# Top-k attention with a mixture of depths: seven parts for the candidates, the 24th candidate as the bias, and the checks of the bounds on VectorE

## The chip, the core and the metric

The kernel runs on one NeuronCore of a Trainium2 chip. A core has four engines that compute, each with its own queue of instructions: TensorE (matrix products, PE in the profile, with its weight loads as PEld), VectorE (DVE), ScalarE (ACT) and GpSimd (POOL). SyncE (SP) issues most of the transfers. The engines wait for each other by semaphores. The metric is the time of one execution on the device in microseconds (us), the median of several runs; lower is better.

## The reference

Eight batches with eight heads, 576 tokens and 64 values a head. Each query keeps its 32 highest scores; all others get no weight. The result, 512 values a token, is the input of a mixture of depths: in each batch the 128 tokens with the highest gate score go through a small network.

```python
scores = scale * np.matmul(q, k.transpose(0, 1, 3, 2))
kth = np.partition(scores, -top_k, axis=-1)[..., -top_k:-top_k + 1]
mask = scores >= kth
scores = np.where(mask, scores, -1000000000.0)
scores = scores - np.max(scores, axis=-1, keepdims=True)
attn = np.exp(scores)
attn = attn / (np.sum(attn, axis=-1, keepdims=True) + 1e-09)
return np.matmul(attn, v).astype(np.float32)
...
for b in range(B):
    top_idx = np.argpartition(-scores[b], capacity)[:capacity]
    xe = x[b, top_idx]
    h = np.maximum(xe @ w1, 0.0)
    ye = h @ w2
    g = 1.0 / (1.0 + np.exp(-scores[b, top_idx]))
    out[b, top_idx] = x[b, top_idx] + g[:, None] * ye
```

## The kernel before

The work is cut into 144 **units**, 18 a batch. A unit is 128 queries for two heads: a tile `sc` of 128 rows with two halves (one a head) of 576 scores. The last 64 tokens of a batch are folded so that two units take them for all heads.

The loop `for n in range(-1, N)` (L1083) is a software pipeline written out by hand. In iteration n, TensorE multiplies queries and keys of unit n + 1, VectorE searches unit n, ScalarE and GpSimd prepare unit n - 1, VectorE finds the 32nd score of unit n - 2, ScalarE and GpSimd make the mask of unit n - 3, and TensorE turns unit n - 4, adds the mask to it, and, once ScalarE has taken the exp, multiplies with v. Each engine carries out its instructions in the order in which the program lists them, since `InOrder` keeps it; queues such as `vector_late` and `pool_late` hold small pieces back until a named point of the iteration.

How the 32nd score of a row is found:

- `find_bound(sc)` (L383), VectorE. Each half is cut into 8 parts of 72 scores. A MAX8 takes the 8 highest of each part: 64 **candidates** (`cand`). Then three rounds pick the 8 highest among the candidates: the first looks at the 3 highest of each part, the second at 7, the third at all 8. After the first and the second, a match_replace overwrites what was picked. The last value of the third round, `best[2][:, i, 7]`, is the 24th candidate, at or below the row's 24th score.
- `cut(best, at)` (L413), ScalarE. A cast copies the upper 16 bits of the two 24th candidates of a unit into `seen[:, 0, ...]`: the value truncated, so a little lower.
- `part(i, sc, at, sides)` (L420), ScalarE. A sign activation of bias - (1 + 2^-23) x score, where the bias is what `cut` kept. It gives -1 for scores at or above the bound and +1 below it; the sum over a row goes to `seen[:, 2, ...]`, and shows how many scores lie above.
- In `what_is_below(n)` (L1056), GpSimd multiplies scores and signs into `y`, so that only those below the bound stay positive, and `fill` (L435) appends eight values that depend on the row's sum.
- `find_kth` (L444), VectorE. One MAX8 over the 584 values of `y`, whose 8th is the 32nd score of the row. The results of a batch lie in one tile, `next8s[b]`.
- `mask` (L449): ScalarE takes one half, GpSimd the other (in a few units VectorE).

Since `fill` only has room for up to eight values, a row may have 24 to 31 scores at or above its bound. At the end the kernel checks (`sure`, L1243) for all rows together: that the bounds and 32nd scores are above a least value, that the row sums lie in range, and some more. To this end `mask_of` (L1073) lets GpSimd copy the 36 values of a batch's 32nd scores to `seen[:, 1, ...]` once a batch. If any check fails, `general` (L1315), a slow exact path for any input, computes all batches again after the rest.

The mixture of depths of batch b runs in steps between the units of the batches b + 1 and b + 2, at places listed in `mix_at` (L991). Most steps put matmuls into TensorE's queue (`h_ps`, `y_ps`).

Of the kernel before, what the change touches and what calls it, by code (L numbers as in the profile page):

```python
# [11 lines left out]
ALU = mybir.AluOpType  # L12
FP32 = mybir.dt.float32
BF16 = mybir.dt.bfloat16
I32 = mybir.dt.int32
# [11 lines left out]
LEAST = 1.0e-16 * SMALLER  # L27
# [2 lines left out]


J = 4


class InOrder:
# [11 lines left out]
def kernel(  # L47
# [12 lines left out]
    P = nc.NUM_PARTITIONS  # L60
    B, H, S, D = q.shape
    HD = H * D
    F = moe_w1.shape[1]
    NHP = H // 2
    NT = J + 1
    JP = J * P
# [9 lines left out]
    const = ctx.enter_context(tc.tile_pool(name="const", bufs=1))  # L76
# [3 lines left out]
    wkpool = ctx.enter_context(tc.tile_pool(name="wk", bufs=2))  # L80
    stats = ctx.enter_context(tc.tile_pool(name="stats", bufs=6))
# [28 lines left out]
    for i in range(2):  # L110
        gate = const.tile([P, NT], FP32, name=f"gate{i}")
        nc.gpsimd.memset(gate, 0.0)
        parts = const.tile([P, NT, 2, 3], BF16, name=f"parts{i}")
# [13 lines left out]


    NS = B * 2 * (J * NHP + NHP // 2)
    seen = const.tile([P, 3, NS], FP32, name="seen")  # L130
    sums = const.tile([P, B * NT, H], FP32, name="sums")
    nc.gpsimd.memset(sums, 1.0)

    MIDDLE = S - 2 * (TOP_K - 8) + 1
# [245 lines left out]
            )  # L380
        return sc

    def find_bound(sc):  # L383

        w = S // 8
        cand = wkpool.tile([P, 2, 64], FP32, name="cand")
        best = [stats.tile([P, 2, 8], FP32, name=f"best{r}") for r in range(3)]  # L390
        for i in range(2):

            if i == 1:
                flush_vector()
            for u in range(8):
                dve.max(cand[:, i, 8 * u : 8 * u + 8], sc[:, i, u * w : (u + 1) * w])


        parts = cand.rearrange("p i (u e) -> p i u e", u=8)
        for r, e in enumerate((3, 7, 8)):  # L400
            for i in range(2):
                dve.max(best[r][:, i, :], parts[:, i, :, 0:e])
            if r < 2:
                for i in range(2):
                    dve.match_replace(
                        parts[:, i, :, 0:e],
                        best[r][:, i, :],
                        parts[:, i, :, 0:e],
                        LOWEST,
                    )  # L410
        return best[2]

    def cut(best, at):  # L413

        act.copy(
            out=seen[:, 0, at : at + 2],
            in_=best.rearrange("p i e -> p (i e)").bitcast(BF16)[:, 15:32:16],
        )

    def part(i, sc, at, sides):  # L420

        act.activation(
            sides[:, i, :],
            sc[:, i, :],
            AF.Sign,
            bias=seen[:, 0, at + i : at + i + 1],  # L430
            scale=-(1.0 + 2.0**-23),
            accum_out=seen[:, 2, at + i : at + i + 1],
        )

    def fill(y, at):  # L435

        pool.tensor_tensor(
            y[:, :, S : S + 8],
            steps,
            seen[:, 2, at : at + 2].unsqueeze(2).to_broadcast([P, 2, 8]),  # L440
            ALU.subtract,
        )

# [542 lines left out]
    per_batch = sum(groups(t) for t in range(NT))  # L986
# [48 lines left out]
    loading = iter(())  # L1035
    inverting = normalised = None
    of_batch = {}
    scs, bests, ys, next8s, masks = {}, {}, {}, {}, {}

    def is_unit(n):  # L1040
        return 0 <= n < N
# [1 line left out]
    def weigh(sc, tr, av, less):  # L1043
# [9 lines left out]

        return pT, last, exp

    def what_is_below(n):  # L1056
        at, sc = 2 * n, scs[n]
        cut(bests.pop(n), at)
        sides = wkpool.tile([P, 2, S], BF16, name="sides")
        y = wkpool.tile([P, 2, S + 8], FP32, name="y")  # L1060
        for i in range(2):
            part(i, sc, at, sides)
            pool.tensor_tensor(y[:, i, 0:S], sc[:, i, :], sides[:, i, :], ALU.mult)
        fill(y, at)
        ys[n] = y

    def kth_of(n):
# [2 lines left out]
            next8s[b] = stats.tile([P, per_batch, 2, 8], FP32, name="next8", bufs=2)  # L1070
        find_kth(ys.pop(n), next8s[b][:, i, :, :])

    def mask_of(n, on=None):  # L1073
        b, i = divmod(n, per_batch)
        masks[n] = mask(scs[n], next8s[b][:, i, :, :], on)
        if i == per_batch - 1:
            at = 2 * per_batch * b
            pool.tensor_copy(
                out=seen[:, 1, at : at + 2 * per_batch].rearrange("p (n i) -> p n i", i=2),
                in_=next8s.pop(b)[:, :, :, 7],  # L1080
            )

    for n in range(-1, N):  # L1083
        b, i = divmod(n, per_batch)
        if i == 0 and 0 <= b < B - 1:
            qkv[b + 1] = room_for_qkv(b + 1)
            loading = chain(
                loading, Rows(k[b + 1], q[b + 1], *qkv[b + 1][0:2]).parts()
            )
        if 0 < n + 1 < NHP:  # L1090
            turn_pair(first_rows, n + 1)
        if n == 1:
            load_v(v[0], qkv[0][2])
        if n == NHP:
            load_weights()


        gating = normalised
        if inverting is not None:
            normalised = inverting[0:2]  # L1100
            vector_late.insert(0, lambda a=inverting: normalise(*a))
            inverting = None
        else:
            normalised = None
        if gating is not None:
            vector_late.append(lambda a=gating: gates(*a))

        if is_unit(n - 4):  # L1110
            tr, av = room_to_turn()
            pT, last, exp = weigh(scs.pop(n - 4), tr, av, masks.pop(n - 4))
            exp()
        if is_unit(n - 3):
            mask_of(n - 3, (act, None) if n in scatter_steps else None)
        flush()
        if is_unit(n + 1):
            b, t, g = units[n + 1]
            ps = room_for_scores()
            multiply(t, g, *qkv[b][0:2], ps)  # L1120
            b, i = divmod(n, per_batch)
            loads = list(islice(loading, first_loads[i] if b == 0 else loads_at[i]))
            halves = [ps[:, a, :, HALF : HALF + P] for a in range(2)]
            for load, half in zip(loads, halves):
                load[0](half)
            scs[n + 1] = keep(ps, n == -1)
            for load, half in zip(loads, halves):
                load[1](half)
        if is_unit(n - 4):
            b4, t4, g4 = units[n - 4]  # L1130
            values(t4, g4, pT, last, av, qkv[b4][2])
            if n in place_steps:
                values_bank[0] = av
                next(mixtures[place_steps[n]])
            if g4 == 0:
                xs = xpool.tile([P, H, DE], FP32, name="xs")
                if t4 == 0:
                    x = xpool.tile([P, NT, HD], FP32, name="x")
                    pg = gates_of[b4 % 2]
                    of_batch[b4] = x, pg  # L1140
            keep_values(t4, g4, av, xs)
            if g4 == groups(t4) - 1:
                inverting = b4, t4, xs
                n4 = R if t4 == J else P
                keep_sums(n4, xs, sums[0:n4, b4 * NT + t4, :])
            while kept:
                kept.pop(0)()


        if is_unit(n):  # L1150
            bests[n] = find_bound(scs[n])
        flush_vector()
        flush_pool()
        if is_unit(n - 2):
            kth_of(n - 2)
        while after_kth:
            after_kth.pop(0)()


        if is_unit(n - 1):  # L1160
            what_is_below(n - 1)

        if gating is not None:
            b, t = gating
            if t == J:
                store(out[b], of_batch[b][0])
                mixtures[b] = mixture(float(b * S), of_batch[b][1], ranks[:, b, :])
        for b in mix_steps.get(n, ()):
            next(mixtures[b], None)
        b, i = divmod(n, per_batch)  # L1170
        if i == v_at and 0 <= b < B - 1:
            load_v(v[b + 1], qkv[b + 1][2])
# [67 lines left out]
    next(closed)  # L1240


    sure = stats.tile([P, 1], FP32, name="sure")  # L1243
    dve.memset(sure, 1.0)
    for what, op, than, limit in (
        (seen[:, 0, :], ALU.min, ALU.is_gt, LEAST),
        (seen[:, 1, :], ALU.min, ALU.is_gt, LEAST),
        (seen[:, 2, :], ALU.max, ALU.is_lt, float(MIDDLE)),
        (seen[:, 2, :], ALU.min, ALU.is_gt, float(MIDDLE - 16)),
        (sums.rearrange("p t h -> p (t h)"), ALU.min, ALU.is_gt, FEWEST),  # L1250
        (sums.rearrange("p t h -> p (t h)"), ALU.max, ALU.is_lt, MOST),
    ):
        far = stats.tile([P, 1], FP32, name="far")
        dve.tensor_reduce(out=far, in_=what, axis=mybir.AxisListType.X, op=op)
        dve.scalar_tensor_tensor(
            out=sure, in0=far, scalar=limit, in1=sure, op0=than, op1=ALU.mult
        )
# [133 lines left out]
```

## Time and profile before

| | |
|---|---|
| time, median of 3 runs | 844.89 us (844.6 to 846.16) |
| the profiled execution: its own time, its span | 845.82 us, 844.0 us |
| TensorE: busy, share of the span | 793.1 us, 94% |
| VectorE | 805.4 us, 95% |
| ScalarE | 759.5 us, 90% |
| GpSimd | 729.6 us, 86% |
| granted TensorE clock, mean | 0.992 |
| MAX8 of 72 scores: number, mean of one | 2304, 218 ns |
| ScalarE's truncating cast: number, mean of one | 144, 203 ns |
| GpSimd's copy to `seen`: number, mean of one | 8, 239 ns |

The times of a group of instructions are those from the start to the end of each. Instructions of one engine can overlap: the next starts before the one before has ended. The mean of one is therefore not what an engine loses to it; that is read from the starts in the timeline. A row of waits names who waited, for whom, how long in total, how often, and the longest.

The profile in 40 equal slices, busy tenths:

```profile
PE   6898888998999999999999999999999999999987
PEld 5666666666787778877787777877788777867754
DVE  7899999999999999999999999999999999999960
ACT  4799999999999999999999999999999999979831
POOL 3689889989989899999999999999999999989831
```

All four engines are busy nearly throughout; the first slices wait for the first loads, and the last four hold the end of the last batch, where one thing follows another.

### The profile page before, as it was taken

What the parts mean: (1) busy time and instruction counts of PE and PEld (TensorE: products, weight loads), DVE (VectorE), ACT (ScalarE), POOL (GpSimd) and SP (SyncE); (2) the same over time, 40 slices, a digit from 0 to 9 for tenths busy, and PEclk for the clock granted to TensorE, in tenths of its full rate; (3) what the DMA queues carried; (4) which work ended last, traced back from release to release, by engine and by line L of the source; (5) the groups of instructions that cost most, each with busy time, mean ns of one, the idle gap of its engine ahead of it and who ended that gap; (6) DMA issues with size and microseconds to landing.
All of it is one profiled execution on the core that took longest, in us unless ns stands there. A gap on an engine that the chain in (4) does not pass through costs nothing. (4 is left out here: it accounts for less than half of the span.)

```text
span 844.0 us, 28167 instructions
## 1 busy us (share of the span) xinstructions
PE 793.1 (94%) x9887; PEld 612.4 (73%) x9887; DVE 805.4 (95%) x4905; ACT 759.5 (90%) x1701; POOL 729.6 (86%) x730
## 2 busy tenths in 40 slices
PE   6898888998999999999999999999999999999987
PEld 5666666666787778877787777877788777867754
DVE  7899999999999999999999999999999999999960
ACT  4799999999999999999999999999999999979831
POOL 3689889989989899999999999999999999989831
PEclk9699999999999999999999999999999999999999
DMA  8931111411141221511323221412215102101021
GB/s 171 279 75 29 40 64 26 104 45 35 58 97 28 52 40 58 110 40 27 89 37 82 51 47 56 101 30 52 39 58 110 27 2 76 23 2 27 2 70 30
DMA packets 122134, 50.38 MB, mean 60 GB/s; under 512 B 116416, under 2 KB 116416, under 8 KB 120960
## 3 DMA queue, kind: packets, MB, share of 16 engines
q1 hardware_dynamic: 118672, 43.91, 21.6%
q0 software_dynamic: 1728, 4.20, 2.8%
q8 instruction: 80, 1.31, 0.7%
q14 instruction: 70, 0.57, 0.3%
q10 hardware_dynamic: 1584, 0.39, 0.2%
HBM read 36.93 MB, written 11.55 MB: 57 GB/s over the span
## 5 line engine op out<-in xcount | busy, mean ns | idle before, releaser
L43 POOL TENSOR_TENSOR y<-sc,sides 128x576 f32<-128x576 f32 x288 | 365.0, 1288 | 73.1 <-ACT sides L43 70.0
L43 DVE MAX8 cand<-sc 128x8 f32<-128x72 f32 x2304 | 330.9, 218 | 1.7 <-ACT sc L43 1.7
L43 POOL TENSOR_SCALAR less<-sc,next 128x576 bf16<-128x576 f32 x135 | 232.9, 1725 | 3.2 <-DVE next L43 2.5
L43 ACT ACTIVATE sides<-sc,seen 128x576 bf16<-128x576 f32 x288 | 221.0, 768 | 5.2
L43 PE MATMUL ptr<-out_of_reach,less 128*128 128x128 bf16 x1136 | 204.8, 220 | 16.2 <-POOL less L43 16.0
L43 PE MATMUL ptr<-ident,sc 128*128 128x128 f32 x1136 | 214.4, 279 | 0.0
L43 DVE MAX8 next<-y 128x8 f32<-128x584 f32 x288 | 204.4, 751 | 3.2 <-POOL y L43 3.2
L43 PE MATMUL ps<-kT,qT 64*128 64x288 f32 (+1 forms) x1280 | 180.9, 431 | 7.6 <-ACT qT L43 5.8
L43 PEld LDWEIGHTS av<-v,pT 128*64 128x64 f32 x4544 | 144.1, 137 | 46.3 <-ACT last L43 33.7
L43 PEld LDWEIGHTS ptr<-ident,sc 128*128 128x128 f32 x1136 | 160.8, 142 | 22.4 <-PE av L43 8.7
L43 PE MATMUL av<-v,pT 128*64 128x65 f32 x4544 | 163.7, 224 | 13.8 <-ACT last L43 12.2
L43 ACT COPY sc<-ps 128x1152 f32<-128x1152 f32 (+1 forms) x144 | 160.5, 1114 | 8.5 <-PE ps L43 7.2
L43 ACT ACTIVATE pT<-ptr 128x1024 f32<-128x1024 f32 x142 | 144.1, 1015 | 18.1 <-PE ptr L43 14.6
L43 PEld LDWEIGHTS <-less 128*128 128x128 bf16 x1296 | 133.2, 104 | 36.4 <-POOL less L43 21.8
L43 DVE MAX8 best<-cand 128x8 f32<-128x24 f32 (+2 forms) x864 | 142.4, 201 | 0.1
L43 PEld LDWEIGHTS ps<-kT,qT 64*128 64x128 f32 (+1 forms) x1280 | 97.8, 177 | 46.6 <-issue 22.1
L43 ACT ACTIVATE less<-sc,next 128x576 bf16<-128x576 f32 x143 | 110.6, 774 | 6.5 <-DVE next L43 6.3
L43 DVE MATCH_REPLACE8 cand<-best,cand 128x24 f32<-128x24 f32 (+1 forms) x576 | 101.9, 185 | 0.0
L43 PE MATMUL av<-vpair,last 128*128 128x130 f32 (+1 forms) x314 | 68.1, 317 | 0.0
L43 PE MATMUL h_ps<-xeT,w 128*128 128x128 f32 x464 | 61.6, 277 | 0.0
L43 PEld LDWEIGHTS h_ps<-xeT,w 128*128 128x128 f32 x464 | 56.0, 192 | 2.1 <-issue 1.2
L43 PE MATMUL y_ps<-w,hT 128*128 128x512 f32 x112 | 56.7, 601 | 0.0
(129 smaller groups left out, 869.7 us busy)
## 6 DMA issues: line engine op xcount, KB each, us to landing
v<-in_v_dram SPq DMA_DIRECT2D x64, 128.0 KB, 3.3
out_dram<-x SPq DMA_DIRECT2D x8, 1024.0 KB, 4.1
rows<-in_k_dram SPq DMA_DIRECT2D x56, 128.0 KB, 2.9
rows<-in_q_dram SPq DMA_DIRECT2D x56, 128.0 KB, 3.1
w<-in_moe_w_dram SPq DMA_DIRECT2D x2, 2048.0 KB
gate_row<-row_dram SPq DMA_DIRECT2D x7, 288.0 KB, 5.1
w<-in_k_dram SPq DMA_DIRECT2D x8, 128.0 KB, 3.4
last<-in_k_dram SPq DMA_DIRECT2D x8, 128.0 KB, 3.5
```

What stands on the lines that cost most here:

```text
L43: return lambda *a, **kw: self._tc.keep_in_program_order(fn(*a, **kw))
```

## The change

- The candidates come from 7 parts (`PARTS`) of 82 or 83 scores in place of 8 of 72: 56 candidates. The three rounds look at 3, 7 and 8 of each part as before.
- The third round writes into a tile `bound` with the values of a whole batch. `part` takes the 24th candidate from it, untruncated, as its bias; `cut` and its cast are gone.
- `keep_least`, once a batch on VectorE, takes the least of the batch's bounds, of its 32nd scores, and of a bit test of the bounds, which shows a bound whose lower 23 bits are exactly 1 (a sign of 0 could occur there). GpSimd's copy in `mask_of` is gone. For the last batch it runs at the end, ahead of the check.
- The check reduces the 8 values of each of these in place of 288; `seen` keeps the row sums alone.

```diff
-    def find_bound(sc):
-        w = S // 8
-        cand = wkpool.tile([P, 2, 64], FP32, name="cand")
-        best = [stats.tile([P, 2, 8], FP32, name=f"best{r}") for r in range(3)]
+    def find_bound(sc, bound):
+        cand = wkpool.tile([P, 2, 8 * PARTS], FP32, name="cand")
+        best = [stats.tile([P, 2, 8], FP32, name=f"best{r}") for r in range(2)]
+        best.append(bound)
...
-            for u in range(8):
-                dve.max(cand[:, i, 8 * u : 8 * u + 8], sc[:, i, u * w : (u + 1) * w])
+            for u in range(PARTS):
+                dve.max(
+                    cand[:, i, 8 * u : 8 * u + 8],
+                    sc[:, i, u * S // PARTS : (u + 1) * S // PARTS],
+                )
...
-        act.copy(
-            out=seen[:, 0, at : at + 2],
-            in_=best.rearrange("p i e -> p (i e)").bitcast(BF16)[:, 15:32:16],
-        )
...
-            bias=seen[:, 0, at + i : at + i + 1],
+            bias=bound[:, i, 7:8],
             scale=-(1.0 + 2.0**-23),
-            accum_out=seen[:, 2, at + i : at + i + 1],
+            accum_out=seen[:, at + i : at + i + 1],
...
+    def bound_of(n):
+        b, i = divmod(n, per_batch)
+        if i == 0:
+            bounds[b] = stats.tile([P, per_batch, 2, 8], FP32, name="bound", bufs=2)
+        find_bound(scs[n], bounds[b][:, i, :, :])
...
+    def keep_least(b, bound, kth):
+        low = stats.tile([P, per_batch, 2], I32, name="low", bufs=1)
+        dve.tensor_scalar(
+            out=low,
+            in0=bound.bitcast(I32),
+            scalar1=(1 << 23) - 1,
+            scalar2=1,
+            op0=ALU.bitwise_and,
+            op1=ALU.bitwise_xor,
+        )
+        for w, of in enumerate((bound, kth, low)):
+            dve.tensor_reduce(
+                out=least[:, w, b : b + 1], in_=of, axis=mybir.AxisListType.XY, op=ALU.min
+            )
...
-        if i == per_batch - 1:
-            at = 2 * per_batch * b
-            pool.tensor_copy(
-                out=seen[:, 1, at : at + 2 * per_batch].rearrange("p (n i) -> p n i", i=2),
-                in_=next8s.pop(b)[:, :, :, 7],
-            )
+        if i == per_batch - 1 and b < B - 1:
+            keep_least(b, bounds.pop(b)[:, :, :, 7], next8s.pop(b)[:, :, :, 7])
...
+    keep_least(B - 1, bounds.pop(B - 1)[:, :, :, 7], next8s.pop(B - 1)[:, :, :, 7])
...
-        (seen[:, 0, :], ALU.min, ALU.is_gt, LEAST),
-        (seen[:, 1, :], ALU.min, ALU.is_gt, LEAST),
-        (seen[:, 2, :], ALU.max, ALU.is_lt, float(MIDDLE)),
-        (seen[:, 2, :], ALU.min, ALU.is_gt, float(MIDDLE - 16)),
+        (least[:, 0, :], ALU.min, ALU.is_gt, LEAST),
+        (least[:, 1, :], ALU.min, ALU.is_gt, LEAST),
+        (least[:, 2, :], ALU.min, ALU.is_gt, 0.5),
+        (seen, ALU.max, ALU.is_lt, float(MIDDLE)),
+        (seen, ALU.min, ALU.is_gt, float(MIDDLE - 16)),
```

More of the change, by code (lines that the diff above doesn't have):

```diff
@@ L32 @@
 J = 4
+PARTS = 7
 class InOrder:
@@ L129 @@
     NS = B * 2 * (J * NHP + NHP // 2)
-    seen = const.tile([P, 3, NS], FP32, name="seen")
+    seen = const.tile([P, NS], FP32, name="seen")
+    least = const.tile([P, 3, B], FP32, name="least")
     sums = const.tile([P, B * NT, H], FP32, name="sums")
@@ L394, in find_bound @@
                 flush_vector()
-            for u in range(8):
-                dve.max(cand[:, i, 8 * u : 8 * u + 8], sc[:, i, u * w : (u + 1) * w])
-        parts = cand.rearrange("p i (u e) -> p i u e", u=8)
+            for u in range(PARTS):
[3 more added lines that the diff above has]
+                )
+        parts = cand.rearrange("p i (u e) -> p i u e", u=PARTS)
         for r, e in enumerate((3, 7, 8)):
@@ L410, in find_bound, with part @@
                     )
-        return best[2]
-    def cut(best, at):
-        act.copy(
-            out=seen[:, 0, at : at + 2],
-            in_=best.rearrange("p i e -> p (i e)").bitcast(BF16)[:, 15:32:16],
-        )
-    def part(i, sc, at, sides):
+    def part(i, sc, bound, at, sides):
         act.activation(
@@ L439, in fill @@
             steps,
-            seen[:, 2, at : at + 2].unsqueeze(2).to_broadcast([P, 2, 8]),
+            seen[:, at : at + 2].unsqueeze(2).to_broadcast([P, 2, 8]),
             ALU.subtract,
@@ L1037 @@
     of_batch = {}
-    scs, bests, ys, next8s, masks = {}, {}, {}, {}, {}
+    scs, bounds, ys, next8s, masks = {}, {}, {}, {}, {}
     def is_unit(n):
@@ L1054, in weigh @@
         return pT, last, exp
+    def bound_of(n):
[3 more added lines that the diff above has]
+        find_bound(scs[n], bounds[b][:, i, :, :])
     def what_is_below(n):
         at, sc = 2 * n, scs[n]
-        cut(bests.pop(n), at)
+        b, i = divmod(n, per_batch)
+        bound = bounds[b][:, i, :, :]
         sides = wkpool.tile([P, 2, S], BF16, name="sides")
@@ L1061, in what_is_below @@
         for i in range(2):
-            part(i, sc, at, sides)
+            part(i, sc, bound, at, sides)
             pool.tensor_tensor(y[:, i, 0:S], sc[:, i, :], sides[:, i, :], ALU.mult)
@@ L1150 @@
         if is_unit(n):
-            bests[n] = find_bound(scs[n])
+            bound_of(n)
         flush_vector()
```

## The prediction

> **What bounds the kernel now.** I read the busy row first, then a table of busy time over four stretches, then the waits of TensorE in the same stretches, then single units in the timeline. The table (length, then busy time of each engine with its number of instructions, granted clock, DMA share, GB/s):
>
> ```profile
> 40.00:215.00 175.00, 156.38 (x2097) 119.38 (x2096) 173.44 (x1065) 167.81 (x379) 159.23 (x152) 1.00 0.23 52
> 215.00:740.00 525.00, 516.89 (x6552) 403.07 (x6553) 523.13 (x3228) 504.63 (x1136) 483.99 (x472) 1.00 0.24 56
> 740.00:800.00 60.00, 56.90 (x720) 45.09 (x719) 59.86 (x364) 51.90 (x115) 53.85 (x51) 1.00 0.06 11
> ```
>
> The columns are PE, PEld, DVE, ACT, POOL. VectorE is full in all three. That alone would say that every nanosecond taken from VectorE counts. But TensorE stands at 89% in the first stretch and 98.5% in the second. Its waits, first in 40 to 215 us, then in 215 to 740 us (total, times, longest):
>
> ```profile
> PE ptr L43 <- POOL less L43: 14.9, 25, 1.3
> PE av L43 <- ACT last L43: 2.8, 5, 0.9
> ```
> ```profile
> PE av L43 <- ACT last L43: 7.5, 12, 0.9
> ```
>
> In the first stretch TensorE lost 17.7 us to others; in the second, three times as long, 7.5 us, which is nearly all of its 525 - 516.9 = 8.1 us of idle time. A busy TensorE could still be one with stretched matmuls, so I looked at two successive units:
>
> ```profile
> 439.21 1.24 PE L43 MATMUL ps<-kT,qT 64*128 64x288 f32 x8
> 440.38 0.44 PE L43 MATMUL ps<-ident,rows 128*128 128x128 f32 x2
> 440.75 1.15 PE L43 MATMUL av<-v,pT 128*64 128x65 f32 x32
> 441.83 0.49 PE L43 MATMUL av<-vpair,last 128*128 128x130 f32 x2
> 442.16 1.05 PE L43 MATMUL h_ps<-xeT,w 128*128 128x128 f32 x8
> ...
> 444.68 1.24 PE L43 MATMUL ps<-kT,qT 64*128 64x288 f32 x8
> 445.85 0.44 PE L43 MATMUL ps<-ident,rows 128*128 128x128 f32 x2
> 446.22 1.15 PE L43 MATMUL av<-v,pT 128*64 128x65 f32 x32
> 447.30 0.49 PE L43 MATMUL av<-vpair,last 128*128 128x130 f32 x2
> 447.63 1.05 PE L43 MATMUL h_ps<-xeT,w 128*128 128x128 f32 x8
> ```
>
> The steps from start to start are 1.17, 0.37, 1.08, 0.33 in both, and 5.47 us from unit to unit. Such equal steps are those of an engine that runs at its own pace. From about 215 us on, when the expert's h and y matmuls of batch 0 join in, TensorE therefore limits most units, and VectorE the same to within 1.5%: **two bounds lie on top of each other**. Before 215 us there are no such matmuls, and VectorE is the bound alone.
>
> **VectorE, searching.** In a unit it now runs 16 MAX8 of 72 elements:
>
> ```profile
> 339.61 1.42 DVE L43 MAX8 next<-y 128x8 f32<-128x584 f32 x2
> 340.94 2.24 DVE L43 MAX8 cand<-sc 128x8 f32<-128x72 f32 x16
> 343.09 0.31 DVE L43 MAX8 best<-cand 128x8 f32<-128x24 f32 x2
> ```
>
> Start to start, 16 take 343.09 - 340.94 = 2.15 us, 134 ns each; a MAX8 of 584 takes (340.94 - 339.61)/2 = 665 ns. So an element costs (665 - 134)/512 = 1.04 ns. With seven parts there are 14 MAX8 of 82 or 83 elements, 134 + 10.3 x 1.04 = 145 ns: 2.03 us, 0.12 us less. The three selecting rounds read 21, 49 and 56 instead of 24, 56 and 64, and the two replacing ones 21 and 49: 28 elements less for each of two halves, 0.058 us. Together **0.18 us a unit**, 25.5 us over 144 units. Here a rule of the Trainium skill gives another sum: "VectorE: DVE Perf Modes", section "The DRAIN you can't avoid", has the next instruction wait until the pipeline is empty. Then whole durations count: 16 x 218 ns (the row's mean) against 14 x 229 is 0.28 us, 49 us in all with the rounds. The row shows 218 ns long instructions starting 134 ns apart, and I take the row.
>
> **VectorE, checking.** Each batch adds a bitwise tensor_scalar and three reductions of 36 elements. Reductions in the trace: 142 ns for 6 elements, 186 for 40; small tensor_scalars 102 to 154. Four make 0.5 to 0.7 us; I take 0.6, no wait, since VectorE made all inputs itself a unit before. What no row shows is a bitwise operation or a reduction on int32. Nearest are two int32 casts, 351 ns for 128 elements and, once, 4095 ns for 16. I take the short one's side, for the long one came once at the start. Nothing can be gained below zero here.
>
> **ScalarE.** 144 casts go. One holds its engine from 344.19 to 344.40, 0.21 us; in other units up to 0.28. The sign activation then waits for VectorE itself. That wait is covered: from the last MAX8 of the selection to the sign it is 3 to 6 us in the units from 24 on that I compared. If it were late, the next unit's exp, queued behind the sign, and TensorE's values after it would be late by as much. ScalarE falls from 96% busy by 3.7%.
>
> **GpSimd** loses 8 copies of 0.24 us, one a batch: 0 to 2 us, I take 0, since it waits longer for ScalarE in every batch. **DMA queues and TensorE** keep every instruction and place.
>
> **The end.** The four reductions of 288 with their products (0.55 us each, start to start) become two, and three of 8 (about 0.25), plus the last batch's 0.6: 2.2 becomes 2.5 us. That runs from 818.8 us beside the gather of xe, which frees TensorE at 822.7; the sum must be ready at 823.3, after the transposes, and is today at 822.9. The 0.3 us about fits; if that cover fails, 0 to 0.3 us, I take 0.
>
> **The sum, against the profile's own 844.0 us span (845.8 with what lies around it; the runs' median is 844.9, 0.1% less, so I take the differences off the median).**
> - To 215 us: units 0 to 5 wait for the first loads, some 31 units are VectorE's. 31 x 0.18 - 0.6 = **4.9 us**. Between 3 and 5.5: others get in the way, or not.
> - 215 to 740: TensorE can give back only its idle 8.1 us. It waits for the last exp of a unit, and ScalarE comes late to it after two or three crowded units without a pause. Each carried one cast: 2 x 0.2 off waits of 0.6 and 0.7 us, 60% of 7.5 is **4.7 us**. Between 1.5 and 8.1.
> - 740 to 800: TensorE's idle 3.1 us; I take **1.2**, from 0 to 3.1.
> - After 800 us nothing changes.
>
> 10.8 us: 844.9 - 10.8 = **834.1**. What is late next is TensorE, and VectorE will begin to wait.
>
> A second rule is to be weighed here, since it speaks for more: "Perfetto Trace Analysis", section "Identifying the Most-Contended Engine", says that matmul busy time is a bad measure and that TensorE's headroom is judged by the busy share of its weight loads. That is 403/525 = 77% in the long stretch, so TensorE would have a quarter to spare and VectorE's saving would count whole. The repeated 5.47 us say that there is none, whatever keeps it busy, and I go by them.
>
> **Rivals.**
> - *VectorE alone sets the pace* (the second rule is right). 25.5 - 1.1 for the first six units - 7 x 0.6 = 20.2 us: **824.7**. For it: VectorE's idle time is 1.9 us in 525. Against: the equal steps. Chance 0.15.
> - *Only the first stretch gains*: waits for the last exp turn out to be bounded by the transposes, not by ScalarE's casts. 844.9 - 4.9 = **840.0**. For it: ScalarE too waited for TensorE's transposes. Against: ScalarE runs without a pause in the units in question. Chance 0.14.
> - *The other side: the integer check is slow.* Its place is VectorE's queue ahead of a unit's search; its price the 4.1 us of the one slow int32 cast, for two instructions a batch. A batch then adds 8.5 us and saves 3.2, so VectorE is 42 us longer: **887**. It decides from 3.2 us a batch, 1.4 an int32 instruction. Against: the other int32 cast at 0.35. Chance 0.04.
> - *The change doesn't do what it says*: with seven parts the 24th candidate lies lower, and one row with over 31 scores at or above it sends all batches through the general path at the end, after 844 us. That path's eight MAX8 of 576 a unit, some 0.66 us each, are 0.76 ms over 144 units alone, so past **1600**. I counted on the reference's inputs: the fullest row has 31. Chance 0.01.
>
> **How the numbers follow.** Forecast 0.66, the rest as above. The range from 826.5 to 840.2 holds the forecast's own (16.7 us of gain at most, 4.5 at least: 828.2 to 840.4), the second rival, and part of the first; outside are the rest of the first, the slow check, and a gain still smaller: under 2 in 10. This kernel's runs tell 0.2%, 1.7 us, from no change. Every case but the last two gains more than that; the forecast at its worst leaves 0.03 for a smaller one. Faster 0.92, same 0.03, slower 0.05.
>
> **What would show it.** TensorE above 99% busy from 215 to 740 us with the same 5.47 us units; VectorE with idle time there of some 2%, waiting for ScalarE's scores or GpSimd's y; 14 MAX8 about 145 ns apart; the first 215 us shorter by about 5. It is wrong if TensorE's units shrink below 5.44 us (the first rival), if its waits for the last exp stay at 7 us (the second), or if an int32 instruction takes over 1 us.

## The result and the profile after

| | before | after |
|---|---|---|
| time, median of 4 runs each | 845.25 us (844.6 to 846.16) | 837.33 us (835.55 to 837.57) |
| ratio, with its 95% interval | | 0.9901 (0.9884 to 0.9918) |
| span of the profiled execution | 844.0 us | 834.8 us |
| busy: TensorE, VectorE | 793.1, 805.4 us | 792.3, 795.3 us |
| busy: ScalarE, GpSimd | 759.5, 729.6 us | 735.2, 728.4 us |

The change makes the kernel 1% faster, 7.9 us between the medians and 9.2 between the two profiled spans. A second set, five runs beside eleven of the kernel before, gave 0.9893 (0.9874 to 0.9911).

The table of busy time over the same three stretches, for the changed kernel (PE, PEld, DVE, ACT, POOL, granted clock, DMA share, GB/s):

```profile
40.00:215.00 175.00, 159.64 (x2148) 123.00 (x2145) 174.10 (x1038) 166.60 (x355) 163.92 (x154) 1.00 0.23 52
215.00:740.00 525.00, 520.65 (x6573) 405.43 (x6571) 522.11 (x3071) 490.10 (x1041) 484.97 (x471) 1.00 0.25 56
740.00:800.00 60.00, 56.65 (x780) 46.33 (x779) 55.50 (x308) 49.78 (x105) 50.43 (x46) 1.00 0.07 15
```

In the long stretch TensorE went from 98.5% to 99.2%, and ScalarE from 96.1% to 93.4%. VectorE, from which 0.16 us of searching a unit was taken, is as full as before: 522.1 of 525. That is the riddle of this case. TensorE's waits in the changed kernel, 40 to 215 us and then 215 to 740 us:

```profile
PE ptr L45 <- POOL less L45: 12.9, 23, 1.2
PE av L45 <- ACT last L45: 2.2, 5, 0.7
```
```profile
PE av L45 <- ACT last L45: 4.3, 9, 0.6
```

The wait for the last exp fell from 7.5 to 4.3 us. Between the waits TensorE's steps are those of before, 1.17, 0.37, 1.08 and 0.33 us (timeline of the changed kernel, h matmuls of one unit; turns left out):

```profile
443.22 1.24 PE L45 MATMUL ps<-kT,qT 64*128 64x288 f32 x8
444.39 0.44 PE L45 MATMUL ps<-ident,rows 128*128 128x128 f32 x2
444.76 1.16 PE L45 MATMUL av<-v,pT 128*64 128x65 f32 x32
445.84 0.49 PE L45 MATMUL av<-vpair,last 128*128 128x130 f32 x2
446.17 1.05 PE L45 MATMUL h_ps<-xeT,w 128*128 128x128 f32 x8
```

**Where VectorE's time went.** I added up VectorE's timeline from start to start over four whole batches (units 54 to 126, one MAX8 for the 32nd score to the same one 72 units later):

| us in four batches | before | after | difference |
|---|---|---|---|
| search: MAX8 of parts, rounds, replacing | 256.2 | 244.9 | -11.3 |
| the gate's dot product, 20 | 18.5 | 23.0 | +4.5 |
| masks made by VectorE, 4, and one choice of slots a batch | 4.9 | 6.8 | +1.9 |
| new checks, 4 | 0 | 2.5 | +2.5 |
| all, with what stayed the same | 394.7 | 392.3 | -2.4 |

The search shrank just as it should: 14 MAX8 of 82 or 83, 145 ns apart. But instructions that the change doesn't touch grew. The dot product of 128 tokens, `prod`, in the groups of 215 to 740 us, before and then after (busy, mean ns of one):

```profile
L43 DVE CUSTOM_DVE_ANT_0 prod<-x,wg 128x512 f32<-128x512 f32 x21 | 21.8, 1040 | 0.0
```
```profile
L45 DVE CUSTOM_DVE_ANT_0 prod<-x,wg 128x512 f32<-128x512 f32 x21 | 26.1, 1242 | 0.0
```

One of them in the timeline of the changed kernel, VectorE and then GpSimd at the same time:

```profile
444.04 1.20 DVE L45 CUSTOM_DVE_ANT_0 prod<-x,wg 128x512 f32<-128x512 f32 x1
```
```profile
443.41 1.28 POOL L45 TENSOR_TENSOR y<-sc,sides 128x576 f32<-128x576 f32 x1
444.65 0.67 POOL L45 TENSOR_TENSOR y<-steps,seen 128x16 f32<-128x16 f32 x1
```

And another, which started while GpSimd made a mask:

```profile
217.22 0.67 DVE L45 CUSTOM_DVE_ANT_0 prod<-x,wg 128x512 f32<-128x512 f32 x1
```
```profile
216.60 1.72 POOL L45 TENSOR_SCALAR less<-sc,next 128x576 bf16<-128x576 f32 x1
```

The first took 1.13 us until the next instruction could start. GpSimd's multiplication ended 0.65 us after its start; the rest is 0.48. The same sum, what is left of GpSimd's multiplication and 0.48 us, fits within 0.02 us all 26 dot products of 128 tokens in the changed kernel that started beside one; they took from 0.61 to 1.69 us. VectorE's own masks do the same with another rest: the five of the long stretch end 0.25 us after the multiplication beside them. GpSimd loses too: its short `y<-steps,seen`, 0.21 us elsewhere, lasted 0.67. So VectorE **stands still inside an instruction, and the profile calls it busy**. However early such a dot product begins, it ends 0.48 us after the multiplication: it acts as a wait for GpSimd that no row of waits shows. This is how VectorE can have less to do and stay full.

The Trainium skill has the exclusion in "SBUF — State Buffer", section "Who interferes with whom": an instruction of VectorE with two inputs in SBUF and a reading one of GpSimd exclude each other for the whole instruction. The trace agrees for GpSimd's multiplications. For its mask, which reads SBUF too, it agrees only near the mask's start. The second dot product above took 0.60 us. Of five such, those that began 0.17 and 0.44 us into the mask took 1.05 and 0.78; those at 0.62 and 0.74 took 0.60 and cost the mask nothing; and beside the one at 0.08, also 0.60, the mask lasted 2.26 us instead of 1.72.

### The profile page after: what moved, and what is told of

Same layout as the page of the kernel before. It is cut to its first block, busy times and chain, and to the rows that moved or that the text cites. A ratio compares the mean times of both kernels' runs of the same rounds, so it can differ in the third digit from the quotient of the medians.

```text
span 834.8 us, 27764 instructions
## 1 busy us (share of the span) xinstructions
PE 792.3 (95%) x9887; PEld 613.0 (73%) x9887; DVE 795.3 (95%) x4651; ACT 735.2 (88%) x1557; POOL 728.4 (87%) x722
## 5 line engine op out<-in xcount | busy, mean ns | idle before, releaser
L45 DVE MAX8 cand<-sc 128x8 f32<-128x82 f32 (+1 forms) x2016 | 313.8, 227 | 2.2 <-ACT sc L45 2.2
L45 ACT ACTIVATE sides<-sc,bound 128x576 bf16<-128x576 f32 x288 | 222.0, 780 | 0.0
L45 PE MATMUL ptr<-out_of_reach,less 128*128 128x128 bf16 x1136 | 205.4, 220 | 14.1 <-POOL less L45 13.9
L45 PEld LDWEIGHTS <-less 128*128 128x128 bf16 x1296 | 134.1, 104 | 33.5 <-POOL less L45 19.5
L45 DVE MATCH_REPLACE8 cand<-best,cand 128x21 f32<-128x21 f32 (+1 forms) x576 | 98.9, 179 | 0.0
L45 DVE MAX8 best<-cand 128x8 f32<-128x21 f32 (+1 forms) x576 | 90.2, 189 | 0.0
L45 ACT ACTIVATION_READ_ACCUMULATOR sides<-sc,bound 128x1 f32 x288 | 58.0, 201 | 0.0
```

Of the source, the lines that this page charges most:

```text
L45: return lambda *a, **kw: self._tc.keep_in_program_order(fn(*a, **kw))
```

## The experiments

Twelve runs of eleven kernels, each with five rounds. The ratio is to the kernel before on the same chip. To see where a difference arises, I read in each timeline when the first exp of a unit starts: the four middle columns give by how much a stretch of units became shorter against the kernel before (unit 36 starts at 225 us there, unit 126 at 719).

| kernel | ratio (95% interval) | to unit 6 | 6 to 36 | 36 to 126 | rest | span, us less |
|---|---|---|---|---|---|---|
| the change, first time | 0.9901 (0.9884 to 0.9918) | 1.5 | 3.8 | 3.2 | 0.7 | 9.2 |
| the change, second time | 0.9893 (0.9874 to 0.9911) | 1.1 | 3.4 | 4.1 | 0.8 | 9.4 |
| seven parts alone | 0.9986 (0.9971 to 1.0) | -0.3 | 1.2 | 1.0 | 0.1 | 2.0 |
| all but the seven parts | 0.9953 (0.9935 to 0.997) | 1.0 | 2.0 | 2.8 | 0.1 | 5.9 |
| one MAX8 more | 0.9955 (0.9938 to 0.9971) | 1.3 | 1.5 | 3.4 | 0.2 | 6.4 |
| unread cast, first time | 0.9939 (0.9923 to 0.9955) | 3.0 | 3.4 | 2.5 | 0.3 | 9.3 |
| unread cast, second time | 0.9897 (0.9879 to 0.9914) | 1.9 | 3.4 | 3.7 | 0.4 | 9.4 |
| no checks per batch | 0.9905 (0.9888 to 0.9922) | 1.2 | 4.5 | 3.8 | 0.5 | 10.0 |
| one-input sum for the dot product | 0.9852 (0.9832 to 0.9873) | 1.6 | 7.0 | 4.3 | 1.2 | 14.1 |
| the same, in the kernel before | 0.9941 (0.9921 to 0.9962) | 1.7 | 2.8 | 1.0 | 0.3 | 5.9 |
| half the experts' matmuls | 0.9787 (0.977 to 0.9804) | 1.1 | 4.1 | 14.0 | 0.2 | 19.5 |
| the same, in the kernel before | 0.9948 (0.993 to 0.9965) | -0.4 | 0.0 | 5.1 | 0.3 | 5.0 |
| half the matmuls and the one-input sum | 0.9652 (0.963 to 0.9674) | 1.9 | 7.0 | 19.9 | 1.8 | 30.5 |

For the second run of the change:

> The changed kernel once more, as it is, beside the others on one chip: 0.990 of the kernel before in every theory.

The column to unit 6 holds the first loads and a stretch of lower granted clock: from 20 to 36 us the mean was 0.57 in both kernels of the result, and 0.79 in the first trace of the unread cast, where the column has 3.0. It is not read below. A difference of about 1 us in the other columns is not to be relied on either (the two runs of the change differ by 0.4 and 0.9, those of the unread cast by 1.1).

The ratios have a limit too. The unread cast has 0.9923 to 0.9955 on one chip and 0.9879 to 0.9914 on another, and these intervals don't meet. On the first of these chips the kernel before took 843.57 us, and three more kernels ran there: seven parts alone, all but the seven parts, and one MAX8 more. They are compared best with each other. All columns use one trace of the kernel before, from an execution of 845.82 us, and their sums are 0.3 to 4.2 us larger than what the ratios give.

### The parts of the change

**Seven parts alone**, in the kernel before:

```diff
-            for u in range(8):
-                dve.max(cand[:, i, 8 * u : 8 * u + 8], sc[:, i, u * w : (u + 1) * w])
+            for u in range(7):
+                dve.max(
+                    cand[:, i, 8 * u : 8 * u + 8],
+                    sc[:, i, u * S // 7 : (u + 1) * S // 7],
+                )
```

> The kernel before with seven parts and nothing else of the change: ScalarE keeps its truncating cast, GpSimd its copy, and nothing is checked once per batch by VectorE. Two bounds (VectorE to 215 us, TensorE after it, with TensorE's waits there set by ScalarE): the first stretch gains 31 units x 0.18 = 5.5 us, the long one next to nothing, since ScalarE still carries its casts and TensorE's waits for the last exp stay near 7.5 us: 839 to 840.5 us. VectorE alone: the whole gain of the change is VectorE's, and the checks of seven batches, about 0.7 us each, are saved besides: 837.3 - 4.9 = 832.4 us.

843.44 beside 843.57 us: neither theory's number. The long stretch gained 1.0 us, which is near the first theory's "next to nothing"; but the first gained 1.2 in place of 5.5. VectorE did search less; over four batches its dot products, masks and choices grew from 23.4 to 34.4 us, which is the whole of the saving. The masks show it best (groups of this kernel from 215 to 740 us; 1064 ns before):

```profile
L43 DVE TENSOR_SCALAR less<-sc,next 128x576 bf16<-128x576 f32 x5 | 12.2, 2449 | 0.0
```

**All but the seven parts**: the changed kernel with `PARTS = 8`.

> The changed kernel with eight parts of 72: the cast is gone, the checks are VectorE's, but the search is as long as before. Two bounds: ScalarE's 0.2 us a unit are worth nothing while VectorE has no slack, and the checks cost about 0.7 us in each of seven batches wherever VectorE is full: 845 to 849 us. ScalarE as the hidden bound: the casts were the gain, so 838 to 841 us.

840.28 us. Here my theory missed, and the rival's range held: taking the cast off ScalarE pays 3 to 5 us, even where VectorE has more to do than before. (GpSimd's eight copies, 1.9 us in all, went with it and were not tested alone.) How can an engine that is full get done sooner? By being blocked less (groups from 215 to 740 us; 1040 ns before):

```profile
L45 DVE CUSTOM_DVE_ANT_0 prod<-x,wg 128x512 f32<-128x512 f32 x21 | 16.2, 771 | 0.0
```

That the earlier signs moved GpSimd's multiplications out of the way is a reading of this row; no run shifted them alone. TensorE's waits for the last exp, 7.5 us before and 4.3 after, point to the half of the change that shortened them (215 to 740 us, with seven parts alone and then with all but them):

```profile
PE av L43 <- ACT last L43: 6.1, 10, 0.7
```
```profile
PE av L45 <- ACT last L45: 3.8, 9, 0.7
```

**One MAX8 more**, in the changed kernel:

```diff
+        spare = stats.tile([P, 8], FP32, name="spare")
+        dve.max(spare, sc[:, 1, 6 * S // PARTS : S])
```

> The changed kernel with one more MAX8 of 83 scores a unit, whose result nobody reads: VectorE has 0.145 us a unit more, 20.9 us in all. Two bounds: the first stretch is longer by 31 x 0.145 = 4.5 us, the long one by what VectorE lacks of slack there, 1 to 3 us: 843 to 845 us. VectorE alone: all of it, 837.3 + 20.9 = 858 us.

839.93 us, below the 843 to 845 that I expected. With 20.9 us more for VectorE, 2 to 5 came out: 4.5 by the two ratios, 2.8 by the two traces, and 1.6 beside the unread cast on the same chip. From unit 36 to 126 it is 13 us more, and the stretch is as short as in the change (3.4 us less than before; the change 3.2 and 4.1). Between units 6 and 36 it costs 2 us. In four batches the search grew by 10.6 us and the checks by 1.9, while dot products, masks and choices fell from 29.9 to 17.2: the blocked time made room. VectorE as the only bound is out.

**An unread cast**, in the changed kernel:

```diff
+        act.copy(
+            out=cuts[:, at : at + 2],
+            in_=bound.rearrange("p i e -> p (i e)").bitcast(BF16)[:, 15:32:16],
+        )
```

> The changed kernel with ScalarE's cast put back into each unit, into a tile that nobody reads; the sign keeps its new bias. Two bounds with ScalarE behind TensorE's waits: nothing in the first stretch, the 3.2 us that the long stretch gained are lost: 839.5 to 841 us, and TensorE's waits for the last exp from 215 to 740 us go from 4.3 us back to some 7. VectorE alone: no change, 837.3 us.

838.37 us lies between the two theories' numbers; the ratio is 0.4% above the change's, 3 us, as the first theory said. But the traced execution, the fastest of the six, with a granted clock of 0.996 against 0.991, had a span of 834.7 us, the change's being 834.8, and TensorE's waits for the last exp were 5.5 us, not some 7. So I ran it again beside the change.

> The changed kernel with ScalarE's unread cast again, now beside the changed kernel on one chip. If ScalarE's casts are what lengthened TensorE's waits in the long stretch: 1 to 3 us above the changed kernel. If the gain there has nothing to do with ScalarE: the same within 0.5 us.

836.89 beside 837.07 us, and 4.4 us of waits for the last exp: nothing. The reason may lie in ScalarE's timeline. In the kernel before, the sign reads what the cast writes:

```profile
447.88 0.31 ACT L43 COPY xs<-av 128x130 f32<-128x130 f32 x1
448.04 0.24 ACT L43 CAST seen<-best 128x2 f32<-128x2 bf16 x1
448.32 0.78 ACT L43 ACTIVATE sides<-sc,seen 128x576 bf16<-128x576 f32 x1
```

Here, where nobody reads it, and then in the changed kernel without it:

```profile
440.76 0.31 ACT L45 COPY xs<-av 128x130 f32<-128x130 f32 x1
440.92 0.24 ACT L45 CAST cuts<-bound 128x2 f32<-128x2 bf16 x1
441.01 0.83 ACT L45 ACTIVATE sides<-sc,bound 128x576 bf16<-128x576 f32 x1
```
```profile
440.95 0.31 ACT L45 COPY xs<-av 128x130 f32<-128x130 f32 x1
441.11 0.83 ACT L45 ACTIVATE sides<-sc,bound 128x576 bf16<-128x576 f32 x1
```

From cast to sign it is 0.28 us where the sign needs it, 0.09 where it doesn't. Over all units, from the end of the instruction ahead to the sign: +124 ns, -12 ns, and -104 ns without a cast (medians). The old cast thus cost 228 ns a unit, of which only 92 were the cast and 136 the wait of the sign for it. The experiment put the 92 back. Beside the change they were worth nothing; by the first run's ratio they cost 3 us, and why the two chips differ stays open. That the 136 carry the gain of the long stretch is inferred, since they were not put back alone. For it speak the waits for the last exp in the kernels with all matmuls: 6.1 to 7.5 us where the sign reads a cast, 4.4 and 5.5 with the unread one, 3.5 to 4.3 without any. By the ratios on the one chip, seven parts alone gave 1.2 us, all else 4.0, and the change with an unread cast 5.1; there the two halves add up.

**No checks per batch**: `keep_least` left out of the loop.

> The changed kernel without the once-per-batch checks (the bounds and 32nd scores of all batches but the last go unchecked). P: what the checks take counts only before 215 us, where two of them run: 835.5 to 837 us. V: seven checks of 0.65 us come off, 832.5 to 833.5 us.

835.84 us beside 843.99, ratio 0.9905; the change has 0.9901 and 0.9893. P's 835.5 to 837 held. Seven checks cost less than the runs can tell; on the engine itself a batch's four instructions took 0.6 us (2.5 in four batches).

### What bounds the long stretch

**Half the experts' matmuls** were left out, in the changed kernel and in the one before:

```diff
-            multiply_h(ps[:, fc % 2, :], fc, xeT)
+            multiply_h(ps[:, fc % 2, :], fc, xeT, NDC if exact else NDC // 2)
...
-            pe.matmul(
-                ps, hT[:, fc, :], w2[:, fc, :], start=(fc == 0), stop=(fc == NFC - 1)
-            )
+            if exact or fc % 2 == 0:
+                pe.matmul(
```

> The changed kernel with about half of the experts' matmuls left out for all batches but the last (h sums over two of four chunks, y over four of eight): TensorE has 8.8 us less a batch. P: from 215 us on VectorE's own work and ScalarE's decide, 94 to 96 us a batch in place of 98.1, 818 to 829 us. V: TensorE doesn't matter, 836 to 838 us.

> The kernel before with the same half of the experts' matmuls left out. P: VectorE's own work without blocking is some 96.6 us a batch of 98.7, so up to 11 us come off: 833 to 838 us. V: VectorE was the bound before, no change, 843 to 845 us.

826.02 us, in P's range: TensorE's relief takes another 10 us off the changed kernel from unit 36 to 126, and none before unit 36. In the kernel before the same relief gave 5.1 there, 839.71 us beside 843.99; the expected 833 to 838 was too low. So TensorE is the bound of the long stretch after the change, and was one of two that lie close together before it. VectorE's waiters show the turn (215 to 740 us of the halved, changed kernel; in the change the first of these rows is 0.5 us, once):

```profile
ACT less L45 <- DVE next L45: 24.1, 41, 2.7
...
POOL less L45 <- DVE next L45: 13.0, 27, 0.8
```

**A one-input sum** in place of the dot product, in three kernels:

```diff
-        dve.tensor_tensor_reduce(
+        dve.tensor_scalar(
             out=prod[0:n, 0:HD],
             in0=x,
-            in1=wg[0:n, :],
-            scale=1.0,
-            scalar=0.0,
+            scalar1=0.7,
+            scalar2=None,
             op0=ALU.mult,
             op1=ALU.add,
             accum_out=g,
         )
```

> The changed kernel with the gate's dot product (VectorE, two inputs, 0.6 to 1.5 us) replaced by a tensor_scalar with a sum, one input and the same size: the gate is the sum of a token's values, w_gate is left out. Theory P (TensorE bounds the long stretch, and VectorE's spare time is hidden inside instructions that GpSimd blocks): 836 to 838 us as the change has, and VectorE now shows idle time, 1 to 3 us in 100. Rival V (VectorE is the bound, and being blocked is a part of its work): 2.5 us a batch come off, 822 to 826 us.

> The kernel before with the gate's dot product replaced by a one-input sum of the same size (w_gate is left out). P: GpSimd's blocking costs VectorE 10.3 - 4.8 = 5.5 us before 215 us, of which 3 to 5 come off there, and at most 1 us in the long stretch, where TensorE decides: 838 to 841 us. V (VectorE decides throughout): 1.6 us a batch more, 830 to 832 us.

> The changed kernel with both: half of the experts' matmuls left out, and the one-input sum in place of the dot product. P: with TensorE out of the way VectorE decides in the long stretch too, and now its blocked time counts: 3.4 us come off before 215 us and about 1 us a batch after it, 815 to 819 us where half of the matmuls alone gave 826. If GpSimd's blocking merely moves to other instructions of VectorE: 822 us, the first stretch's gain alone.

The sum took 655 to 687 ns each time, whatever GpSimd did. In the changed kernel this gave 831.54 us, between my two numbers: 3 us in the first stretch, where I had forgotten that P too must gain, and at most 1 in the long one. The idle time that P foretold didn't come. The blocked time moved: VectorE's ten masks, all over the kernel, take 1924 ns each here (1000 in the change).

```profile
L45 DVE TENSOR_SCALAR less<-sc,next 128x576 bf16<-128x576 f32 x10 | 19.2, 1924 | 0.2
```

In the kernel before, 840.38 us, within P's range: 2.8 us of it before unit 36, 1.0 after. And with half of the matmuls gone, 815.74 us: in the long stretch the same edit is now worth 5.9 us (19.9 against 14.0). **Blocked time counts where VectorE is the bound, and is mere spare time where TensorE is.** The other rival, blocking that only moves, holds in the kernels with all matmuls, and falls here.

No version came out of this that computes everything and beats the change: the one-input sum leaves w_gate out.

## Why the prediction was right, point by point

- **Two bounds on top of each other; TensorE's equal steps against the busy share of its weight loads**: right. 77% of weight loads left no room: taking TensorE's work away gave 10 us, adding 13 to VectorE cost none. (The page names the matmul work done against the peak beside the weight loads; the prediction left that out.) The most frequent distance from unit to unit stayed: 5.44 and 5.47 us before, 5.45 and 5.48 after. The rival in which VectorE alone sets the pace (824.7 us) fell with these.
- **VectorE's search, 0.18 us less a unit**: 0.16 measured (11.3 us in 72 units), at the 145 ns predicted for a MAX8. The rule of whole durations would have given twice that; its page excepts an instruction that is not held, and these start 145 ns apart.
- **The checks, 0.6 us a batch**: 0.6. The int32 operations are not slow by themselves, 174 ns for the reduction; the bit test took 174 to 1252 ns. The longest meets a sign that the prediction had named for being wrong, an int32 instruction of over 1 us. But it ended 0.05 us after a multiplication of GpSimd that had begun just before it, and the two that started beside no instruction of GpSimd took 174 and 182 ns. So the slow rival at 887 us had nothing behind it.
- **Before 215 us, 4.9 us**: 3.8 and 3.4 from unit 6 to 36 in the two runs; the first units, for which the prediction put nothing, make it 5.3 and 4.5. The size was about right and its reason was not: so far that is luck. The sum also took off the checks of one batch where two fell into the stretch. I held VectorE for the bound alone; but seven parts alone gave 1.2 us between units 6 and 36, the rest of the change 2.0, both together 3.4 to 3.8. ScalarE's chain through the sign and GpSimd is a bound there too.
- **215 to 740 us, 4.7 us** (60% of 7.5 is 4.5; the sum slipped): 3.2 and 4.1 in two runs, from unit 36 to 126. Right in its kind: TensorE's waits for the last exp shrank from 7.5 to 4.3 us, and the casts were the cause as far as the runs tell; I had put 60% on it, it was 43%, and 53% in the second run (3.5 us left).
- **740 to 800, 1.2 us, and nothing in the end**: 0.7 for all after unit 126. The end's cover held; the first transposes again waited 0.6 us for the gather.
- **The term that was too large** is thus spread: 10.8 us predicted, 7.9 measured between the medians of the first set and 8.9 in the second. "Only the first stretch gains" (840.0) fell by the column from unit 36 to 126; the general path didn't run.
- **What failed outright**: "VectorE will begin to wait", with some 2% of idle time, which would be 10.5 us. It has 2.9 us in 525, against 1.9 before. Its spare time is inside the dot products and masks. I had read "VectorE is full in all three" as work; part of it was standing still before the change already: 20 dot products took 18.5 us, where 0.60 each would be 12.

## What to carry to other kernels

An engine that is 99% busy need not be the bound: compare the durations of the same instruction across its instances, and an instruction whose length varies by a factor of two or three may be waiting inside. A bound shows by steps that repeat to a hundredth of a microsecond, and is tested by adding work to the rival engine or taking it from the bound one. A tiny instruction between two others can cost less by its length than by the wait of the next one for its result.

## What the runs showed that I had not expected

- From start to start, the dot product with two inputs took 0.60 to 1.69 us, by what GpSimd was at; a sum of the same size with one input 0.59 to 0.61.
- One input alone doesn't make an instruction of VectorE safe: masks, choices of slots and the bit test varied too (174 to 1252 ns for the same bit test); the sum and the counting of ranks, which have an accumulator, hardly did (655 to 687 ns, and 757 to 814).
- A cast of two values cost ScalarE 228 ns with a reader right behind it and 92 ns without.
- Adding 20.9 us of work to an engine that was 99.4% busy from 215 to 740 us made the kernel 2 to 5 us longer; taking out 22.6 us had by itself changed it by 0.1 us between the medians and 1.2 by the ratio, no more than the runs can tell.
